# The last layer's first product in Strassen form, with its softplus as one ScalarE function

## The chip, the cores and the metric

The kernel runs on one core of one Trainium2 chip. The metric is the device time of that core in microseconds (us), as the median of several executions. The traces of a profiled execution come from the same core; all times inside a trace count from the first instruction of the span.

## The reference

Three blocks run one after the other. Causal attention (2 batches, 8 heads, 576 positions, head size 64) gives 1152 tokens of 512 numbers. A mixture of eight experts, with weights from an iterated row and column normalisation, follows; each expert is `relu(x @ w1) @ w2` with 1024 hidden columns. The last block is one plain feed-forward layer with 2048 hidden columns and a softplus:

```
def _moe2_ref(x, w_in, w_out):
    h = x @ w_in
    g = np.maximum(h, 0.0) + np.log1p(np.exp(-np.abs(h)))
    return (g @ w_out).astype(np.float32)
```

`x` is 1152 x 512, `w_in` 512 x 2048, `w_out` 2048 x 512. This block and its input are what the change is about.

## The kernel before

**Parts.** Hidden columns are worked in slices of 512, which the code calls layers `x`. The experts are the layers 0 to 15 (`NX` = 16), the last block the layers 16 to 19 (`NH` = 20). A layer has a first product (512 numbers of a token to 512 hidden ones, tile `ph`), an activation (`evict`, to `hh` and `hl`) and a second product (`downs`, tile `py`, accumulated over layers in `acc`).

**Three passes.** Every operand is kept as a high part in the fast matmul type and a low part that holds the rest (`xh`/`xl`, `w1h`/`w1l`, `hh`/`hl`). A product is the sum high x high, high x low, low x high, so each block of a product is three TensorE instructions.

**Experts' first product.** The class `Unit` (L273) works one half `g` of the tokens (576, as two halves of 288 columns) and one half `p` of the hidden columns by Strassen's scheme: seven products `p1` to `p7` of 6 matmuls each (L293), in place of eight. Sums between the products are done by ScalarE copies out of PSUM (L301, `v` and `u`) and VectorE additions (L314, L332, L343). The token columns have seven blocks: `B11`, `B21`, `B22` as they are and `T1` to `T4` as sums; the weights likewise (`sums1`, `sums2` on GpSimd, `split` on ScalarE and VectorE). The experts' eviction is one ScalarE `Relu` (L238) and one VectorE subtraction (L241).

**The last block's first product.** `plain` (L346) makes a hidden block of 128 x 288 by 12 matmuls (L357), four such blocks per `p` and `g`: 48 matmuls where a `Unit` has 42. Its eviction is three ScalarE functions (`Abs`, `Exp`, `Ln`, L253 to L255), two VectorE operations (L259, L260), one on GpSimd (L261), one more on VectorE (L264), then the high part by ScalarE (L267) and the low part by VectorE (L270), put off over the next pieces by `defer` and `flush`.

**Between the two.** The tokens that enter layer 16 are `acc` after layer 15. `turn(g)` (L973) transposes them on TensorE into `px` (L981, L991); ScalarE takes the high part (L983, L992) and VectorE the low part (L985, L994).

**Order.** The work is recorded in the order of strings that `play` reads: `a1` ... `b4` are products of the two units, `p` half a plain block, `d` three matmuls of a second product for one tile of 128 tokens, `=0` to `=2` and `w0` to `w3` start the preparation of the next layer's weights, one step of which follows every piece (`step`). Each engine runs its instructions in that order. Layer `x` plays `A_SEQ` (its own second half of tokens and the second products of tiles 0 to 3), then `B_SEQ` (the next layer's first half, and tiles 4 to 8). From layer 16 on `A_PLAIN` and `B_PLAIN` take their place, and between layers 15 and 16 stands a part of its own, in which `turn(0)` and `turn(1)` are played.

Of the kernel before, what the change touches and what calls it, by code (L numbers as in the profile page):

```python
# [10 lines left out]
F32 = mybir.dt.float32  # L11
# [9 lines left out]
def attention_moe_ffn(ctx, tc, q, k, v, s, w_gate, w1, w2, w_in, w_out, out):  # L21
# [148 lines left out]
    def prep1(x, g):  # L170
# [3 lines left out]
        if g == 0:  # L174
            if x < NX:
                for p in range(2):
                    yield from sums1(x, p)
            for p in range(2):
                yield from split(x, p, 0, [(slice(0, 2), slice(2, 4))])
            if x < NX:  # L180
                for p in range(2):
                    yield from sums2(x, p)
        elif g == 1:
            for p in range(2):
                yield from split(x, p, 1, [(slice(0, 2), slice(1, 3) if x < NX else slice(1, 5, 3))])
                if x >= NX:
                    load(x + 1, 1, p)
        elif x < NX:
# [23 lines left out]
    m3_t = []  # L212
# [20 lines left out]
    def evict(x, k, z, q, cols):  # L233

        hh, hl = hb[0][:, q, cols], hb[1][:, q, cols]
        if x < NX:
# [12 lines left out]
        m3 = m3_t[-1]  # L249
        a1 = m3.tile([P, HB], F32, tag="a1", name="a1")  # L250
        a2 = m3.tile([P, HB], F32, tag="a2", name="a2")
        a3 = m3.tile([P, HB], F32, tag="a3", name="a3")
# [4 lines left out]
        def sums():  # L257

            nc.vector.tensor_scalar(a2, a1, 1.0, -1.0, ALU.add, ALU.add)  # L259
            nc.vector.scalar_tensor_tensor(out=a3, in0=z, scalar=0.0, in1=a3, op0=ALU.max, op1=ALU.add)  # L260
            nc.gpsimd.tensor_tensor(out=a2, in0=a1, in1=a2, op=ALU.subtract)  # L261

        def total_():
            nc.vector.tensor_tensor(out=a3, in0=a3, in1=a2, op=ALU.add)  # L264

        def high():
            nc.scalar.activation(out=hh, in_=a3, func=AF.Copy)  # L267

        def rest_():
            nc.vector.tensor_tensor(out=hl, in0=a3, in1=f(hh), op=ALU.subtract)  # L270

        defer(1, sums)
        defer(3, total_)  # L273
        defer(5, high)
        defer(7, rest_)

# [68 lines left out]

    def plain(x, p, g, i, j):  # L346

        o = ps.tile([P, 512], F32, tag="sc", name="ph", bufs=4)[:, :HB]
        wh, wl = wt[x, 1, p, i]
        ops = []  # L350
        for r in range(2):
            for c in range(2):
                k = slice(c * P, (c + 1) * P)
                h, l = xh[g][:, 2 * r + c, j, :], xl[g][:, 2 * r + c, j, :]
                ops += [(wh[:, r, k], h), (wh[:, r, k], l), (wl[:, r, k], h)]
        for n, (u, v) in enumerate(ops):
            nc.tensor.matmul(o, u, v, start=(n == 0), stop=(n == 11))  # L357
            if n == 5:
                flush()
                yield  # L360
        flush()
        evict(x, 0, o, p + 2 * i, slice(g * S + j * HB, g * S + (j + 1) * HB))
        yield
# [43 lines left out]
    with tc.manual_schedule():  # L407
# [565 lines left out]
        def turn(g):  # L973
# [186 lines left out]
```

## Time and profile before

| what | value |
|---|---|
| median of three runs | 1088.02 us (1087.88 to 1089.03) |
| profiled execution, its own time | 1087.74 us |
| its span, first to last instruction | 1086.0 us |
| TensorE busy | 1071.4 us (99%) |
| VectorE busy | 772.9 us (71%) |
| ScalarE busy | 521.9 us (48%) |
| GpSimd busy | 359.9 us (33%) |
| granted TensorE clock | 0.999 of full speed |

The span is 1.74 us shorter than the profiled execution's time, and that execution lies 0.28 us under the median. Matmuls overlap each other in the trace (one of 288 columns has a duration of 0.30 us, and the next starts 0.13 us after it), so the length of a row of matmuls is read from starts, or from the chain of waits, which merges a row of equal ones to one piece with its length.

### The profile page before, as it was taken

What the parts mean: (1) busy time and instruction counts of PE and PEld (TensorE: products, weight loads), DVE (VectorE), ACT (ScalarE), POOL (GpSimd) and SP (SyncE); (2) the same over time, 40 slices, a digit from 0 to 9 for tenths busy, and PEclk for the clock granted to TensorE, in tenths of its full rate; (3) what the DMA queues carried; (4) which work ended last, traced back from release to release, by engine and by line L of the source; (5) the groups of instructions that cost most, each with busy time, mean ns of one, the idle gap of its engine ahead of it and who ended that gap; (6) DMA issues with size and microseconds to landing.
All of it is one profiled execution on the core that took longest, in us unless ns stands there. A gap on an engine that the chain in (4) does not pass through costs nothing.

```text
span 1086.0 us, 18114 instructions
## 1 busy us (share of the span) xinstructions
PE 1071.4 (99%) x6684; PEld 944.5 (87%) x6684; DVE 772.9 (71%) x1731; ACT 521.9 (48%) x1239; POOL 359.9 (33%) x429
## 2 busy tenths in 40 slices
PE   7999999999999999999999999999999999999998
PEld 4777889889898888988888898888889898989896
DVE  5576556767877878787887888775455568687774
ACT  7998444334443433434343343434333365566661
POOL 8785303053332415134241523423020032323231
PEclk9999999999999999999999999999999999999999
DMA  5221111122232222223222231411112111111002
GB/s 195 85 76 55 40 40 39 40 86 97 92 126 89 85 98 97 94 75 134 83 83 97 98 95 71 136 59 40 39 39 68 50 40 40 39 40 40 1 11 77
DMA packets 30384, 78.43 MB, mean 72 GB/s; under 512 B 5728, under 2 KB 10848, under 8 KB 30296
## 3 DMA queue, kind: packets, MB, share of 16 engines
q1 hardware_dynamic: 27552, 68.69, 18.7%
q0 software_dynamic: 2560, 8.39, 2.0%
q8 instruction: 52, 0.85, 0.3%
q14 instruction: 36, 0.29, 0.1%
q10 hardware_dynamic: 184, 0.20, 0.1%
HBM read 65.99 MB, written 10.75 MB: 71 GB/s over the span
## 4 chain that ended last, share of the span: by engine, by line
PE 93%; DVE 3%; ACT 2%; POOL 1%; issue 1%; DMA 0%; SPq 0%; POOLq 0%; ACTq 0%; DVEq 0%
PE py L382 46%; PE ph L293 32%; PE ph L357 9%; PE sc L598 1%; PE pv L705 1%; PE tr L679 1%; ACT eb L648 1%; POOL eb L661 1%; PE sc L602 0%; PE tr L673 0%; PE pv L715 0%; PE pg L885 0%; ACT pt L693 0%; PE tr L685 0%; PE px L991 0%
## 5 line engine op out<-in xcount | busy, mean ns | idle before, releaser
L382 PE MATMUL py<-w2h,hh 128*128 128x512 f32 x720 | 285.8, 397 | 0.1
L382 PE MATMUL py<-w2h,hl 128*128 128x512 f32 x720 | 284.8, 396 | 1.0 <-DVE hl L241 1.0
L382 PE MATMUL py<-w2l,hh 128*128 128x512 f32 x720 | 284.5, 395 | 0.0
L293 PE MATMUL ph<-xh,w1h 128*128 128x288 f32 x896 | 265.2, 296 | 0.2 <-ACT v L301 0.2
L293 PE MATMUL ph<-xh,w1l 128*128 128x288 f32 x896 | 264.8, 296 | 0.0
L293 PE MATMUL ph<-xl,w1h 128*128 128x288 f32 x896 | 263.4, 294 | 0.0
L293 PEld LDWEIGHTS ph<-xh,w1h 128*128 128x128 f32 x896 | 168.0, 187 | 17.5 <-ACT v L301 0.5
L293 PEld LDWEIGHTS ph<-xl,w1h 128*128 128x128 f32 x896 | 168.3, 188 | 16.5
L293 PEld LDWEIGHTS ph<-xh,w1l 128*128 128x128 f32 x896 | 168.2, 188 | 0.0
L382 PEld LDWEIGHTS py<-w2h,hl 128*128 128x128 f32 x720 | 135.2, 188 | 33.9 <-DVE hl L241 1.6
L238 ACT ACTIVATE hh<-ph 128x288 fp32r<-128x288 f32 x192 | 78.6, 411 | 161.0 <-DVE ph L343 82.2
L204 POOL TENSOR_TENSOR w2l<-raw,w2h 128x512 fp32r<-128x512 f32 x40 | 56.0, 1400 | 290.7 <-ACT w2h L202 290.7
L382 PEld LDWEIGHTS py<-w2h,hh 128*128 128x128 f32 x720 | 135.1, 188 | 12.7 <-DVE acc L400 0.6
L382 PEld LDWEIGHTS py<-w2l,hh 128*128 128x128 f32 x720 | 135.3, 188 | 11.6
L301 ACT ACTIVATE v<-ph 128x288 f32<-128x288 f32 x128 | 50.8, 410 | 172.6 <-PE ph L293 169.7
L400 DVE SCALAR_TENSOR_TENSOR acc<-py,gate,acc 128x512 f32<-128x512 f32 x126 | 94.0, 746 | 53.2 <-PE py L382 53.1
L968 POOL TENSOR_TENSOR cm<-cm,ct 128x512 f32<-128x512 f32 x32 | 45.1, 1408 | 202.5 <-DVE ct L966 202.5
L152 DVE TENSOR_TENSOR w1l<-raw,w1h 128x512 fp32r<-128x512 f32 (+1 forms) x144 | 98.3, 683 | 15.2 <-ACT w1h L149 15.1
L241 DVE SCALAR_TENSOR_TENSOR hl<-ph,hh 128x288 fp32r<-128x288 f32 x192 | 86.7, 454 | 30.7 <-ACT hh L238 29.0
L261 POOL TENSOR_TENSOR a<-a,a 128x288 f32<-128x288 f32 x64 | 51.7, 808 | 125.0 <-DVE a L259 119.8
L149 ACT ACTIVATE w1h<-raw 128x512 fp32r<-128x512 f32 (+1 forms) x144 | 83.0, 576 | 1.6 <-PE ph L293 1.6
L357 PE MATMUL ph<-xh,w1h 128*128 128x288 f32 x256 | 76.0, 297 | 0.0
(191 smaller groups left out, 1692.1 us busy)
## 6 DMA issues: line engine op xcount, KB each, us to landing
raw<-in_w SPq DMA_DIRECT2D x64, 512.0 KB
f<-in_w_in SPq DMA_DIRECT2D x16, 512.0 KB
f<-in_w_out SPq DMA_DIRECT2D x16, 512.0 KB
wd<-cm POOLq DMA_DIRECT2D x32, 256.0 KB, 3.1
raw<-wd SPq DMA_DIRECT2D x16, 512.0 KB
out<-acc SPq DMA_DIRECT2D x9, 256.0 KB
vv<-in_v SPq DMA_DIRECT2D x8, 256.0 KB
qk<-in_k SPq DMA_DIRECT2D x7, 288.0 KB
```

Of the source, the lines that this page charges most:

```text
L149: nc.scalar.activation(out=hi[:, o], in_=t[:, src], func=AF.Copy)
L152: nc.vector.tensor_tensor(out=lo[:, o], in0=t[:, src], in1=f(hi[:, o]), op=ALU.subtract)
L204: (nc.gpsimd if i else nc.vector).tensor_tensor(out=lo, in0=t[:, r], in1=f(hi), op=ALU.subtract)
L238: nc.scalar.activation(out=hh, in_=z, func=AF.Relu)
L241: nc.vector.scalar_tensor_tensor(out=hl, in0=z, scalar=0.0, in1=f(hh), op0=ALU.max, op1=ALU.subtract)
L261: nc.gpsimd.tensor_tensor(out=a2, in0=a1, in1=a2, op=ALU.subtract)
L293: nc.tensor.matmul(o, u, v, start=(start and c == 0 and n == 0), stop=(c == 1 and n == 2), skip_group_check=True)
L301: nc.scalar.activation(out=t, in_=self.a, func=AF.Copy)
L357: nc.tensor.matmul(o, u, v, start=(n == 0), stop=(n == 11))
L382: nc.tensor.matmul(py[t], u, v, start=(k == 0 and n == 0), stop=(k == NF - 1 and n == 2))
L400: nc.vector.scalar_tensor_tensor(out=a, in0=py, scalar=gate_t[0][:, t, e:e + 1], in1=a, op0=ALU.mult, op1=ALU.add)
L968: nc.gpsimd.tensor_tensor(out=m, in0=m, in1=f(t), op=ALU.add)
```

## The change

The four layers of the last block use `Unit` as the experts do, and `plain` with its two sequences is gone. `evict` for these layers is a `Softplus` of ScalarE in place (in PSUM, or in the tile `t`), a ScalarE `Copy` to `hh` and a VectorE subtraction to `hl`. A table set with softplus is loaded once, ahead of layer 14. `turn` builds seven blocks per half `g` and is cut in two: its first part (`t`) transposes into a tile `xq` and makes `B11` and `B21`, its second (`u`) the sums `T1` to `T4` and `B22`. The sequence `TURN` plays these among layer 15's second products and layer 16's first ones, and `A_TURN` follows it. The preparation of the weights treats all layers alike.

```diff
@@ prep1 @@
-            if x < NX:
-                for p in range(2):
-                    yield from sums1(x, p)
+            for p in range(2):
+                yield from sums1(x, p)
...
@@ evict @@
         hh, hl = hb[0][:, q, cols], hb[1][:, q, cols]
-        if x < NX:
-            def high():
+
+        def high():
+            if x < NX:
                 nc.scalar.activation(out=hh, in_=z, func=AF.Relu)
-
-            def rest_():
+            else:
+                nc.scalar.activation(out=z, in_=z, func=AF.Softplus)
+                nc.scalar.activation(out=hh, in_=z, func=AF.Copy)
+
+        def rest_():
+            if x < NX:
                 nc.vector.scalar_tensor_tensor(out=hl, in0=z, scalar=0.0, in1=f(hh), op0=ALU.max, op1=ALU.subtract)
-
-            if k < 0:
-                high()
             else:
-                defer(k, high)
-            defer(k + 1, rest_)
-            return
...
-        nc.scalar.activation(out=a1, in_=z, func=AF.Abs)
-        nc.scalar.activation(out=a1, in_=a1, func=AF.Exp, scale=-1.0)
-        nc.scalar.activation(out=a3, in_=a1, func=AF.Ln, bias=1.0)
...
+                nc.vector.tensor_tensor(out=hl, in0=z, in1=f(hh), op=ALU.subtract)
+
+        if k < 0:
+            high()
+        else:
+            defer(k, high)
+        defer(k + 1, rest_)
...
@@ turn @@
+        def rows(g, cs, tiles, o):
+
+            n = len(tiles) * P
+            px = ps.tile([P, len(cs), n], F32, tag="tr", name="px", bufs=2)
+            for i, c in enumerate(cs):
+                for j, t in enumerate(tiles):
+                    nc.tensor.transpose(px[:, i, j * P:(j + 1) * P], acc[0][:, t, c * P:(c + 1) * P], ident)
+            nc.scalar.activation(out=xq_t[g][:, cs[0]:cs[-1] + 1, o:o + n], in_=px, func=AF.Copy)
...
+        def both_parts(g, blk, src):
+            h, l = xh[g][:, blk], xl[g][:, blk]
+            for c in range(2):
+                nc.scalar.activation(out=h[:, c, :] if isinstance(blk, int) else h[:, :, c, :], in_=src(c), func=AF.Copy)
+            yield
+            for c in range(2):
+                o = (l[:, c, :], h[:, c, :]) if isinstance(blk, int) else (l[:, :, c, :], h[:, :, c, :])
+                nc.vector.tensor_tensor(out=o[0], in0=src(c), in1=f(o[1]), op=ALU.subtract)
+            yield
+
+        def turn(g, first):
+
+            if first:
+                xq_t[g] = tq_[0].tile([P, KD, S], F32, tag="xq", name="xq", bufs=1)
+            xq = xq_t[g]
+            if first:
+                if g:
+                    rows4(g)
+                    yield
+                for cs in ((0, 1), (2, 3)) if g else ((0,), (1,), (2,), (3,)):
+                    rows(g, cs, (NB + 1, NB + 2) if g else range(NB), REM if g else 0)
+                    yield
+                yield from both_parts(g, B11, lambda c: xq[:, c, :HB])
+                yield from both_parts(g, B21, lambda c: xq[:, c + 2, :HB])
+                return
+            if g:
+                for cs in ((0, 1), (2, 3)):
+                    rows(g, cs, (NB + 3, NB + 4), REM + 2 * P)
+                    yield
+            else:
+                rows4(g)
                 yield
+            xt = [tq_[0].tile([P, 4, HB], F32, tag=f"xt{c}", name="xt", bufs=1) for c in range(2)]
+
+            def sum_(c, n):
+                x1, x2 = xq[:, c, :], xq[:, c + 2, :]
+                o, a, b = [(0, x1[:, HB:], x1[:, :HB]), (1, x2[:, HB:], xt[c][:, 0, :]), (3, x2[:, :HB], xt[c][:, 1, :]),
+                           (2, x2[:, HB:], x1[:, HB:])][n]
+                (nc.gpsimd if n == 3 else nc.vector).tensor_tensor(out=xt[c][:, o, :], in0=a, in1=b, op=ALU.subtract)
+
+            for c in range(2):
+                for n in (3, 0, 1, 2):
+                    sum_(c, n)
+            yield
+            yield from both_parts(g, slice(T2, T3 + 1), lambda c: xt[c][:, 1:3, :])
+            yield from both_parts(g, B22, lambda c: xq[:, c + 2, HB:])
+            for z in (T1, T4):
+                yield from both_parts(g, slice(z, z + 1), lambda c: xt[c][:, z - T1:z - T1 + 1, :])
...
@@ play @@
+                if z[0] in "tu":
+                    side.append(turn(int(z[1]), z[0] == "t"))
+                    continue
...
-        A_PLAIN = "p p p p d d p d p d p d p d =0 p d p d p d p d p d p d p d p =1 d d d"
+        A_TURN = "a1 b1 a2 b2 =0 d d d d a6 d b6 d a7 d b7 =1 d a5 d b5 d a3 d b3 d a4 d b4 d d d"
+        TURN = ("t0 d d d d u0 d d d d d a1 d b1 d a2 d =2 b2 t1 d a6 d b6 d a7 d b7 d a5 d b5 d d u1 w0 a3 w2 b3 w1 a4 w3 b4")
...
-                m3_t.append(ctx.enter_context(tc.tile_pool(name="m3", bufs=6, reuse_waits="tile")))
-            play(A_SEQ if x < NX else A_PLAIN, products(x, 1), downs(x, A_GROUPS))
+                nc.scalar.preload_act_table_set("softplus")
+            play(A_SEQ if x != NX else A_TURN, products(x, 1), downs(x, A_GROUPS))
...
+            if x + 1 == NX:
+                tq = ctx.enter_context(tc.tile_pool(name="tq", bufs=1, reuse_waits="tile"))
+                tq_.append(tq)
+                play(TURN, products(NX, 0), d)
+            elif x + 1 < NH:
                 play(B_SEQ, products(x + 1, 0), d)
...
```

Three places show how instructions move. On TensorE, where the tokens' transposes begin, before:

```order
L382 MATMUL py<-w2h_9185,hh 128x512
L382 MATMUL py<-w2l_9186,hh 128x512
L382 MATMUL py<-w2h_9185,hl 128x512
L981 MATMUL px<-ident,acc 128x64 x4
L382 MATMUL py<-w2h_9203,hh 128x512
L382 MATMUL py<-w2l_9204,hh 128x512
L382 MATMUL py<-w2h_9203,hl 128x512
L991 MATMUL px<-ident,acc 128x128 x4
```

The same place on TensorE in the changed kernel, just after layer 15's tiles 0 to 3 are complete (L337 is the old L382, L936 the old L991):

```order
L337 MATMUL py<-w2h_9242,hl 128x512
L337 MATMUL py<-w2h_9183,hh 128x512
L337 MATMUL py<-w2l_9184,hh 128x512
L337 MATMUL py<-w2h_9183,hl 128x512
L936 MATMUL px<-ident,acc 128x128 x4
L337 MATMUL py<-w2h_9201,hh 128x512
```

Before, the first transposes are of the shared tile 4 and stand after its second product; now they are of tiles 0 to 3 and stand one `d` into tile 4, whose own transposes come four `d` and more later.

On ScalarE, evictions of the last block before (L253 to L255 softplus, L267 the high part):

```order
L253 ACTIVATE a_10207<-ph 128x288
L254 ACTIVATE a_10207<-a_10207 128x288
L255 ACTIVATE a_10209<-a_10207 128x288
L267 ACTIVATE hh<-a_10175 128x288
L253 ACTIVATE a_10239<-ph 128x288
```

On ScalarE in the changed kernel, from the first blocks of half 0 on (L937 and L946 take transposes to `xq`, L951 a block's high part, L275 the copies `v`, L236 and L237 softplus and high part):

```order
L937 ACTIVATE xq<-px 128x512 x4
L951 ACTIVATE xh_74<-xq 128x288 x4
L946 ACTIVATE xq<-px 128x4x64
L275 ACTIVATE v<-ph 128x288
L951 ACTIVATE xh_74<-xt 128x2x288 x2
L275 ACTIVATE v<-ph 128x288
L951 ACTIVATE xh_74<-xq 128x288 x2
L236 ACTIVATE ph<-ph 128x288
L237 ACTIVATE hh<-ph 128x288
L951 ACTIVATE xh_74<-xt 128x288 x2
```

Four functions per evicted block have become two, and the blocks' high parts stand in the same queue as the first evictions of layer 16.

On VectorE, from the first low part of the tokens on, before:

```order
L985 TENSOR_TENSOR xl_76<-px,xh_74 128x4x64
L994 TENSOR_TENSOR xl_76<-px,xh_74 128x512 x2
L400 SCALAR_TENSOR_TENSOR acc<-py,gate,acc 128x512
L994 TENSOR_TENSOR xl_76<-px,xh_74 128x512 x2
L400 SCALAR_TENSOR_TENSOR acc<-py,gate,acc 128x512
L204 TENSOR_TENSOR w2l_9547<-raw_9230,w2h_9546 128x512
```

The same in the changed kernel (L986 are the sums to `xt`, L955 the low parts, L355 the old L400, L288 the sum in `p2`, L243 the eviction's low part):

```order
L955 TENSOR_TENSOR xl_76<-xq,xh_74 128x288 x2
L355 SCALAR_TENSOR_TENSOR acc<-py,gate,acc 128x512
L955 TENSOR_TENSOR xl_76<-xq,xh_74 128x288 x2
L986 TENSOR_TENSOR xt<-xq 128x288
L986 TENSOR_TENSOR xt<-xq,xt 128x288 x2
L986 TENSOR_TENSOR xt<-xq 128x288
L986 TENSOR_TENSOR xt<-xq,xt 128x288 x2
L955 TENSOR_TENSOR xl_76<-xt,xh_74 128x2x288 x2
L288 TENSOR_TENSOR ph<-ph,v 128x288
L955 TENSOR_TENSOR xl_76<-xq,xh_74 128x288 x2
L355 SCALAR_TENSOR_TENSOR acc<-py,gate,acc 128x512
L243 TENSOR_TENSOR hl<-ph,hh 128x288
```

The sums and the two-block low parts now stand ahead of the addition of `p2` and of the eviction that frees its bank.

## Rows read from the trace of the kernel before

**Rows 1.** The page: busy time, share of the span, instructions.

```profile
PE 1071.4 (99%) x6684; PEld 944.5 (87%) x6684; DVE 772.9 (71%) x1731; ACT 521.9 (48%) x1239; POOL 359.9 (33%) x429
```

**Rows 2.** The page: chain that ended last, shares by line.

```profile
PE py L382 46%; PE ph L293 32%; PE ph L357 9%; PE sc L598 1%; PE pv L705 1%; PE tr L679 1%; ACT eb L648 1%; POOL eb L661 1%; PE sc L602 0%; PE tr L673 0%; PE pv L715 0%; PE pg L885 0%; ACT pt L693 0%; PE tr L685 0%; PE px L991 0%
```

**Rows 3.** Waits of PE and PEld, 820 to 1086 us: total, times, longest.

```profile
PE px L981 <- DVE acc L400: 0.2, 1, 0.2
...
PEld py L382 <- DVE acc L400: 0.6, 1, 0.6
PEld px L981 <- DVE acc L400: 0.6, 1, 0.6
```

**Rows 4.** Waits of PE, 120 to 820 us.

```profile
PE py L382 <- DVE hl L241: 1.0, 1, 1.0
```

**Rows 5.** Chain of waits: start, length; the five products between two expert layers.

```profile
599.60 3.99 PE ph L293 x30
...
837.00 3.99 PE ph L293 x30
```

**Rows 6.** The same, where two layers of the last block meet, and the end.

```profile
941.12 4.76 PE ph L357 x36
...
1042.40 4.76 PE ph L357 x36
...
1065.83 16.11 PE py L382 x69
```

**Rows 7.** Chain of waits, 858 to 872 us, where `turn(0)` is played.

```profile
858.74 4.21 PE py L382 x18
...
862.98 0.76 DVE acc L400
...
863.79 0.46 PE px L981 x4
...
865.14 0.44 PE px L991 x4
...
871.11 0.76 DVE acc L400
...
871.92 0.95 PE py L382 x3
```

**Rows 8.** Instructions that touch tile `ph`: duration ns min/median/max, first and last start.

```profile
L238 ACT ACTIVATE hh<-ph x192: 389/411/415, 111.2 to 859.3; 128x288 fp32r<-128x288 f32 x192
L241 DVE SCALAR_TENSOR_TENSOR hl<-ph,hh x192: 443/454/460, 111.6 to 859.7; 128x288 fp32r<-128x288 f32 x192
```

**Rows 9.** Groups by line and shape, 941.12 to 1042.40 us: busy, mean ns.

```profile
L267 ACT ACTIVATE hh<-a 128x288 fp32r<-128x288 f32 x33 | 14.4, 436 | 18.7 <-DVE a L264 18.7
L255 ACT ACTIVATE a<-a 128x288 f32<-128x288 f32 x32 | 14.3, 445 | 1.0
```

**Rows 10.** VectorE's line L270, whose two inputs lie in SBUF: duration min/median/max.

```profile
L270 DVE TENSOR_TENSOR hl<-a,hh x64: 444/725/1016, 882.2 to 1071.4; 128x288 fp32r<-128x288 f32 x64
```

**Rows 11.** Timeline of VectorE, 893 to 895 us: start, duration.

```profile
893.14 0.45 DVE L264 TENSOR_TENSOR a<-a,a 128x288 f32<-128x288 f32 x1
...
894.09 1.01 DVE L270 TENSOR_TENSOR hl<-a,hh 128x288 fp32r<-128x288 f32 x1
```

**Rows 12.** Timeline of GpSimd, the same stretch.

```profile
893.98 0.81 POOL L261 TENSOR_TENSOR a<-a,a 128x288 f32<-128x288 f32 x1 [1.29 <-DVE a L259]
```

**Rows 13.** Timeline of ScalarE, 0 to 4 us.

```profile
2.46 1.28 ACT L479 ACT_TABLE_LOAD   x1 [2.46 <-issue]
```

**Rows 14.** Timeline of VectorE, 858 to 861 us: end of layer 15's first product.

```profile
858.78 0.47 DVE L343 TENSOR_TENSOR ph<-ph,u 128x288 f32<-128x288 f32 x1
859.73 0.46 DVE L241 SCALAR_TENSOR_TENSOR hl<-ph,hh 128x288 fp32r<-128x288 f32 x1 [0.48 <-ACT hh L238]
860.18 0.75 DVE L400 SCALAR_TENSOR_TENSOR acc<-py,gate,acc 128x512 f32<-128x512 f32 x1
```

**Rows 15.** Windows of an expert layer and of the last block: PE, PEld, DVE, ACT, POOL.

```profile
786.00:829.00 43.00, 43.00 (x253) 38.67 (x252) 21.64 (x42) 15.64 (x36) 8.42 (x10) 1.00 0.14 50
...
958.00:1001.00 43.00, 43.00 (x256) 38.77 (x255) 31.12 (x62) 23.65 (x57) 13.11 (x15) 1.00 0.15 50
```

More of the change, by code (lines that the diff above doesn't have):

```diff
@@ L174, in prep1 @@
         if g == 0:
-            if x < NX:
-                for p in range(2):
-                    yield from sums1(x, p)
+            for p in range(2):
+                yield from sums1(x, p)
             for p in range(2):
                 yield from split(x, p, 0, [(slice(0, 2), slice(2, 4))])
-            if x < NX:
-                for p in range(2):
-                    yield from sums2(x, p)
+            for p in range(2):
+                yield from sums2(x, p)
         elif g == 1:
             for p in range(2):
[L185 to L188, printed above, removed]
+                yield from split(x, p, 1, [(slice(0, 2), slice(1, 3))])
+        else:
             for p in range(2):
@@ L211, in attention_moe_ffn @@
     m_t = []
-    m3_t = []
     hb = []
@@ L344, in p4 @@
             evict(self.x, 0, self.c, self.p + 2, self.h0)
[L346 to L363, printed above, removed]
     def downs(x, groups):
@@ L984, in turn @@
             yield
[L985 removed]
+            for c in range(2):
+                o = (l[:, c, :], h[:, c, :]) if isinstance(blk, int) else (l[:, :, c, :], h[:, :, c, :])
+                nc.vector.tensor_tensor(out=o[0], in0=src(c), in1=f(o[1]), op=ALU.subtract)
             yield
[L987 to L995 removed]
+        def turn(g, first):
[16 more added lines that the diff above has]
+                    yield
+            else:
+                rows4(g)
+                yield
+            xt = [tq_[0].tile([P, 4, HB], F32, tag=f"xt{c}", name="xt", bufs=1) for c in range(2)]
[12 more added lines that the diff above has]
+                yield from both_parts(g, slice(z, z + 1), lambda c: xt[c][:, z - T1:z - T1 + 1, :])
@@ L999, in attention_moe_ffn @@
         back = []
+        side = []
         tick = [0, 0, 0, 0]
@@ L1015, in step @@
                 next(conv, None)
-            while back and next(back[0], 1):
-                back.pop(0)
+            for todo in (back, side):
+                while todo and next(todo[0], 1):
+                    todo.pop(0)
         def rest():
-            for z in back:
-                for _ in z:
-                    pass
-            back.clear()
+            for todo in (back, side):
+                for z in todo:
+                    for _ in z:
+                        pass
+                todo.clear()
         ORDER = "a1 b1 a2 b2 a6 b6 a7 b7 a5 b5 a3 b3 a4 b4"
         def products(x, g):
-            if x < NX:
-                u = dict(a=Unit(x, 0, g), b=Unit(x, 1, g))
-                return {z: getattr(u[z[0]], "p" + z[1]) for z in ORDER.split()}
-            def sums():
-                for i in range(2):
-                    for j in range(2):
-                        for p in range(2):
-                            yield from plain(x, p, g, i, j)
-            z = sums()
-            return {"p": lambda: next(z)}
+            u = dict(a=Unit(x, 0, g), b=Unit(x, 1, g))
+            return {z: getattr(u[z[0]], "p" + z[1]) for z in ORDER.split()}
         def play(seq, todo, d=None):
```

57 lines of the change are left out of this document (5 added, 52 removed).

## The prediction, made before the changed kernel ran

> **What bounds the kernel now.** I read the page's busy shares first: TensorE is busy 99% of the span, no other engine above 71% [rows 1]. The chain that ended last then says whether this is work or overlap: the second products (L382) hold 46% of it, the experts' first product (L293) 32%, the last block's first product (L357) 9%, and no line of another engine more than 1% [rows 2]. TensorE's own waits come third, since a full engine can still stand still at one place. From 120 to 820 us, nearly all of the expert layers, it waited 1.0 us once [rows 4]; from 820 us to the end its queue for weights shows two waits of 0.6 us and its matmuls one of 0.2, all for VectorE's update of `acc`, around the transposes [rows 3]. So from 120 us on the time is TensorE's count of instructions times their pitch. A matmul removed there is worth its pitch, and other work matters only where it makes TensorE wait.
>
> **The gain: 24 matmuls in each of four layers.** A plain half layer has 48 matmuls per `p`, a `Unit` 42, so a layer has 4 x 6 = 24 fewer, four layers 96. I price them in two ways. By the pitch: 36 matmuls of the last block follow each other in 4.76 us, 0.132 each [rows 6], so 96 make 12.7 us. By whole layers, which holds everything that differs between the forms: the piece where two expert layers meet starts at 599.60 and again, five layers on, at 837.00 [rows 5], 47.48 us per layer; the piece where two layers of the last block meet starts at 941.12 and, two layers on, at 1042.40 [rows 6], 50.64 us. The difference, 3.16 us, times four is 12.64 us. I take 12.64. Second products, transposes (40 of them in `turn` before and after) and the last 69 matmuls [rows 6] are the same in both kernels, and so is what follows the last matmul.
>
> **Evictions in the four layers.** Before, a block had four ScalarE functions of about 0.44 us [rows 9], four VectorE operations and one on GpSimd. Now a `Unit` half layer has, as with the experts, four evictions and three copies, and an eviction is two ScalarE functions. No row shows Softplus, nor a ScalarE write into PSUM. Bounds from near rows: `Relu` out of PSUM 0.41, `Ln` 0.445 [rows 8, 9], and as the far end `Abs`, `Exp`, `Ln` together, 1.3 us. I take 0.45, as all ScalarE functions of this size shown lie within 0.04 of each other. The Trainium skill (ScalarE: Activation LUTs, section "Step-by-step: what each stage is for") says that ScalarE takes the same time per element whatever the function; rows 8 and 9 agree for four of them, none shows Softplus.
>
> An expert layer keeps ScalarE busy 15.64 of 43 us [rows 15]. Sixteen extra functions of 0.45 per layer add 7.2, so ScalarE stays near half full. What counts is the longer chain at the end of a layer's first product. In layer 15 the last matmul of `b4` ends about 858.74 [rows 7]; VectorE adds at 858.78, then `Relu`, and the low part is done at 859.73 + 0.46 = 860.19 [rows 14]. One more function makes it 860.65. Its first reader is the fourth `d` of tile 4, two `d` of tile 3 and three of tile 4 after `b4`: 858.74 + 5 x 0.70 = 862.24, with 0.70 for three matmuls (16.11 us for 69, [rows 6]). So 1.5 us of cover is left of 2.0, and I price it at nothing. Without that cover it would be one stall per layer of the length by which the chain is late.
>
> **The table load.** One more load of a ScalarE table, ahead of layer 14; a load took 1.28 us at the start [rows 13]. Behind it ScalarE has the last `Relu` of the layer before and the copies `v`, which `a6` needs: three products of 0.79 and two `d` later, 3.8 us. Price nothing; on the path it would be at most 1.28.
>
> **The turn, where the cost is.** Before, `turn(0)` cost TensorE two stops: its matmul queue was at work until about 863.48 and the first transpose came at 863.79; the last weight before 871.92 had gone out by 871.61 [rows 7]. That is 0.3 us each, 0.6 in all, and both places go: the first transposes now wait only for tile 3, whose update ends at 860.93 [rows 14], while one `d` from 859.98 runs to 860.68; and the paired group of tiles 7 and 8 that waited for a bank of `py` is two single groups. What comes late next is the handing on of blocks. I lay them out from `t0` at 859.98:
>
> - Four `d` with four sets of transposes (0.44 each, [rows 7]), five more `d` and the small set: `a1` starts about 868.5. `B11` and `B21` are two ScalarE functions and two VectorE ones each; they queue from 865.2 on and are done about 867.3. No wait.
> - The sums start with the copy of the small set, 868.8: six on VectorE, two on GpSimd, then low parts of two blocks at once. `a6` reads them four products and three to four `d` after 868.5, at about 874.4. At 0.45 a VectorE operation (starts 0.37 apart) they are done at 872.6.
> - But all six read two SBUF tiles while GpSimd reads SBUF too. L270, of the same kind, has a minimum of 444 and a median of 725 ns [rows 10], and one beside a GpSimd operation of 0.81 [rows 12] took 1.01 where its neighbour took 0.45 [rows 11]: 0.56 more per meeting, 1.1 us for two, up to 1.6 if the two engines take strict turns. Then the low parts are done at 873.7 to 874.2, just ahead of `a6`, and the additions and evictions of `a2` and `b2` queue behind them; these free the two PSUM banks that the next two sets of transposes take. By this reckoning TensorE stops three times, 0.4 to 0.5 each.
>
> The Trainium skill (SBUF — State Buffer, section "Who interferes with whom") says that a VectorE instruction with two SBUF inputs and a GpSimd instruction that reads SBUF exclude each other. By it each meeting would cost VectorE up to the whole 0.81, 3.2 us for the turn's four GpSimd sums; by rows 11 it is 0.56, 2.2 us. I go by the rows; the rule speaks for the high end of the stalls.
>
> As a check, VectorE's whole work in `TURN`, counted from the order: 38 operations of 288 columns (0.45), two of 576 (at most 0.9), some eight of 512 (0.75) and two small ones: 25.6 us, with the meetings up to 27.8. TensorE has 20 `d`, 14 products and ten sets of transposes, 14.0 + 11.1 + 4.4 = 29.5 us. VectorE is nearly full, in part waiting for ScalarE in order, so some stops are likelier than none. Bounds for them: nothing, and 4 us, if each of the ten pairs of low parts in the two halves made TensorE stop for 0.4. I take 1.4, the three stops of the layout. Half 1 has more cover: its `B11` stands ready long before `a1`, and four `d` in a row stand before `a6`.
>
> **Sum.** Against the profiled execution: 1087.74 - 12.64 - 0.6 + 1.4 = 1075.9. The median is 0.28 above that execution, so 1076.2 is the forecast.
>
> **Rivals.**
>
> 1. *VectorE becomes the bound in the turn.* For it: 27.8 of 29.5 us, and rows 10 with over half of such operations stretched. Against it: the work is spread, and the late blocks (`T1`, `T4`, `B22`) have five products of cover. If the stops reach 4 to 7 us in the two halves, the time is 1088.02 - 12.64 - 0.6 + 4 to 7 = 1079 to 1082.
> 2. *The longer eviction chain shows at every seam.* For it: 0.45 of 2.0 us of cover goes, and ScalarE has weight splits in the same queue. Against it: experts' layers ran with no wait [rows 4]. If each of seven seams lost 0.5 to 1 us: 3.5 to 7 us more, 1079.7 to 1083.
> 3. *Softplus is slow and ScalarE becomes the bound; slower than before.* An expert layer has 47.48 us; ScalarE needs about 15.64 x 47.48/43 = 17.3 of it, and 7.2 for the second functions. What is left, 23 us over 16 evictions, is 1.4 us each: from 1.9 us per function on, a layer is ScalarE's. To eat 12.64 us over four layers takes 3.2 us more per layer, so about 2.1 us per function; at 2.5 us the time is 1076.2 + 64 x 0.6 = 1115. Against it: every function shown takes 0.41 to 0.445, and the order has one table load, not one per function.
> 4. *The change doesn't do what it says*: the products are 42, but the copies and sums between them stop TensorE, so that a layer stays near 50.6 us. Against it stands the expert layers' 47.48 us in the same code. It would end near 1088.
>
> **How the numbers follow.** What this kernel's measurement can tell from no change is about 0.2%, 2.2 us. The forecast gets 0.80, with a range of its own from 1074.7 (no stop at all: 1088.02 - 12.64 - 0.6) to 1078.8 (stops of 4 us). Rival 1 gets 0.10, rival 2 0.05, rival 3 0.03, rival 4 0.01; 0.01 is left for a gain beyond the count. The range 1074.5 to 1079.0 leaves out most of rivals 1 to 4. All but rivals 3 and 4 are faster by over 0.2%: faster 0.96, within 0.2% 0.01, slower 0.03.
>
> **What would show it.** The seams of layers 16 to 19 should be 47.5 us apart; Softplus about 0.45 us; TensorE's waits should stand only between 860 and 890 us, below 3 us in all, on VectorE (banks, low parts) or ScalarE (`xq` copies) before `px`; GpSimd's sums there should go with VectorE sums stretched to about 1 us. The forecast is wrong if seams of the last layers lie over 48 us apart, or if the waits in the turn exceed 4 us.

## The result, and the profile after

The changed kernel took 1078.16 us, the median of 4 runs (1078.05 to 1079.39), against 1087.95 (1087.88 to 1089.03, 4 runs) for the kernel before: ratio 0.991, 95% interval 0.9893 to 0.9927. It is 9.8 us faster, where 11.8 were forecast. The profiled execution took 1078.05 us with a span of 1076.3 and a granted clock of 1.0; the sum had said 1075.9, so 2.15 us are missing. Executions of one kernel, of before too, lie in two groups some 1.1 us apart, and in the profiled ones the difference arises ahead of layer 15's seam (836.8 to 838.1 us), so small effects are read below from a stretch behind it.

The page's busy times, answering to [rows 1], and the chain by line, answering to [rows 2]:

```profile
PE 1059.6 (98%) x6588; PEld 931.5 (87%) x6588; DVE 727.7 (68%) x1629; ACT 504.5 (47%) x1200; POOL 336.4 (31%) x401
...
PE py L337 45%; PE ph L267 39%; PE sc L553 2%; PE pv L660 1%; PE tr L634 1%; DVE xt L986 1%; DVE xl L955 1%; PE sc L557 1%; POOL eb L616 1%; PE tr L628 1%; PE pv L670 0%; PE pg L840 0%; PE tr L640 0%; ACT eb L603 0%; PE px L936 0%
```

TensorE has 96 matmuls fewer, as counted, and is still what the chain consists of. New in the chain are VectorE's `xt` (L986, the sums `T1` to `T4`) and `xl` (L955, the low parts of the tokens): both belong to `turn`.

The chain of waits of the changed kernel at the seams of layers 15, 17, 18 and 19 and at the end (start, length), answering to [rows 5] and [rows 6]:

```profile
836.91 3.99 PE ph L267 x30
...
940.13 3.99 PE ph L267 x30
987.61 3.99 PE ph L267 x30
1035.09 3.99 PE ph L267 x30
...
1056.83 15.41 PE py L337 x66
```

From layer 17 on the seams are 47.48 us apart, where 50.64 stood in [rows 6]. Up to layer 15's seam nothing moved (836.91, before 837.00). The 66 second products at the end have the pitch they had (15.41 us for 66; 16.11 for 69 in [rows 6]). So what is missing was lost between 836.91 and 940.13, in the turn. TensorE's waits there, in its weights' queue (820 to 1077 us; total, times, longest), answering to [rows 3]:

```profile
PEld py L337 <- DVE acc L349: 1.5, 1, 1.5
PEld py L337 <- DVE hl L243: 0.9, 1, 0.9
PEld px L936 <- DVE hl L243: 0.5, 1, 0.5
PEld px L944 <- DVE hl L243: 0.5, 1, 0.5
PEld py L337 <- DVE w2l L200: 0.4, 1, 0.4
PEld px L944 <- issue: 0.4, 1, 0.4
PEld px L936 <- ACT xq L946: 0.3, 1, 0.3
PEld px L936 <- DVE acc L355: 0.2, 1, 0.2
```

The timeline of the weights' queue gives their places (start, duration, in brackets the idle time before and what ended it):

```profile
876.27 0.32 PEld L944 LDWEIGHTS px<-ident,acc 64*128 64x128 f32 x4 [0.51 <-DVE hl L243]
...
878.00 0.42 PEld L936 LDWEIGHTS px<-ident,acc 128*128 128x128 f32 x4 [0.52 <-DVE hl L243]
...
879.26 0.42 PEld L936 LDWEIGHTS px<-ident,acc 128*128 128x128 f32 x4 [0.35 <-ACT xq L946]
...
896.37 0.19 PEld L337 LDWEIGHTS py<-w2h,hl 128*128 128x128 f32 x1 [0.91 <-DVE hl L243]
...
898.67 0.19 PEld L337 LDWEIGHTS py<-w2l,hh 128*128 128x128 f32 x1 [0.41 <-DVE w2l L200]
...
905.93 0.19 PEld L337 LDWEIGHTS py<-w2h,hh 128*128 128x128 f32 x1 [1.49 <-DVE acc L349]
```

Two clusters: three stops at 876 to 879, where half 1's first transposes wait for what half 0's blocks hold up (half 0's stops from here on), which the forecast had; and three at 896 to 906, half 1's, which it had not. They are 1.38 and 2.81 us, 4.19 in all. Two smaller ones, 0.36 us at 868 and 0.20 at 887, make up the rest of the list. The worst, 1.49 us, waits for a copy out of `py` (L349) that stands in VectorE's queue behind half 1's low parts. VectorE there:

```profile
890.81 0.97 DVE L986 TENSOR_TENSOR xt<-xq 128x288 f32<-128x288 f32 x1
891.88 2.35 DVE L986 TENSOR_TENSOR xt<-xq,xt 128x288 f32<-128x288 f32 x2
894.15 0.45 DVE L986 TENSOR_TENSOR xt<-xq 128x288 f32<-128x288 f32 x1
894.64 0.95 DVE L986 TENSOR_TENSOR xt<-xq,xt 128x288 f32<-128x288 f32 x2
...
898.90 1.93 DVE L955 TENSOR_TENSOR xl<-xq,xh 128x288 fp32r<-128x288 f32 x2
900.75 0.45 DVE L288 TENSOR_TENSOR ph<-ph,v 128x288 f32<-128x288 f32 x1
901.12 0.44 DVE L243 TENSOR_TENSOR hl<-ph,hh 128x288 fp32r<-128x288 f32 x1
901.48 1.36 DVE L955 TENSOR_TENSOR xl<-xt,xh 128x288 fp32r<-128x288 f32 x2
...
903.13 1.54 DVE L955 TENSOR_TENSOR xl<-xt,xh 128x288 fp32r<-128x288 f32 x2
904.60 0.68 DVE L152 TENSOR_TENSOR w1l<-raw,w1h 128x512 fp32r<-128x512 f32 x1
905.20 0.68 DVE L349 COPY acc<-py 128x512 f32<-128x512 f32 x1
```

And GpSimd in the same stretch:

```profile
890.66 1.79 POOL L986 TENSOR_TENSOR xt<-xq 128x288 f32<-128x288 f32 x2 [19.58 <-DVE hl L243]
892.41 1.51 POOL L200 TENSOR_TENSOR w2l<-raw,w2h 128x512 fp32r<-128x512 f32 x1
899.22 1.30 POOL L200 TENSOR_TENSOR w2l<-raw,w2h 128x512 fp32r<-128x512 f32 x1 [5.30 <-ACT w2h L198]
900.47 0.96 POOL L158 TENSOR_TENSOR raw<-raw 128x256 f32<-128x256 f32 x1
...
903.52 0.84 POOL L160 TENSOR_TENSOR raw<-raw 128x256 f32<-128x256 f32 x1
```

Each slow VectorE row lies beside a GpSimd row; the two at 894.15 and 894.64, with no GpSimd beside them, take 0.45 and 0.95 for two. With 0.45 for one, 0.95 for a pair of sums and 0.82 for a pair of low parts undisturbed, VectorE lost 0.52 + 1.40 + 1.11 + 0.54 + 0.72 = 4.3 us here. Only operations whose inputs both lie in SBUF are slow here: the two at 900.75 and 901.12 have one input in PSUM (`ph`), lie beside GpSimd too, and take 0.45 and 0.44. That the meetings are what makes TensorE stop is a reading so far; the experiments test it.

### The profile page after: what moved, and what is told of

It is laid out like the page before. It is cut to its first block, busy times and chain, and to the rows that moved or that the text cites. A ratio compares the mean times of both kernels' runs of the same rounds, so it can differ in the third digit from the quotient of the medians.

```text
span 1076.3 us, 17617 instructions
## 1 busy us (share of the span) xinstructions
PE 1059.6 (98%) x6588; PEld 931.5 (87%) x6588; DVE 727.7 (68%) x1629; ACT 504.5 (47%) x1200; POOL 336.4 (31%) x401
## 4 chain that ended last, share of the span: by engine, by line
PE 92%; DVE 4%; ACT 2%; issue 1%; POOL 1%; DMA 0%; POOLq 0%; ACTq 0%; DVEq 0%
PE py L337 45%; PE ph L267 39%; PE sc L553 2%; PE pv L660 1%; PE tr L634 1%; DVE xt L986 1%; DVE xl L955 1%; PE sc L557 1%; POOL eb L616 1%; PE tr L628 1%; PE pv L670 0%; PE pg L840 0%; PE tr L640 0%; ACT eb L603 0%; PE px L936 0%
## 5 line engine op out<-in xcount | busy, mean ns | idle before, releaser
L267 PE MATMUL ph<-xh,w1h 128*128 128x288 f32 x1120 | 331.6, 296 | 0.3 <-ACT v L275 0.3
L267 PE MATMUL ph<-xh,w1l 128*128 128x288 f32 x1120 | 331.0, 295 | 0.0
L267 PE MATMUL ph<-xl,w1h 128*128 128x288 f32 x1120 | 329.2, 294 | 0.0
L337 PE MATMUL py<-w2h,hh 128*128 128x512 f32 x720 | 285.9, 397 | 1.3 <-DVE acc L349 1.3
L337 PE MATMUL py<-w2h,hl 128*128 128x512 f32 x720 | 284.8, 396 | 1.4 <-DVE hl L241 1.0
L337 PE MATMUL py<-w2l,hh 128*128 128x512 f32 x720 | 284.6, 395 | 0.1
L267 PEld LDWEIGHTS ph<-xh,w1h 128*128 128x128 f32 x1120 | 209.9, 187 | 21.7 <-ACT v L275 0.5
L267 PEld LDWEIGHTS ph<-xl,w1h 128*128 128x128 f32 x1120 | 210.3, 188 | 20.6
L267 PEld LDWEIGHTS ph<-xh,w1l 128*128 128x128 f32 x1120 | 210.3, 188 | 0.0
L337 PEld LDWEIGHTS py<-w2h,hl 128*128 128x128 f32 x720 | 135.3, 188 | 34.9 <-DVE hl L241 1.6
L275 ACT ACTIVATE v<-ph 128x288 f32<-128x288 f32 x160 | 63.5, 409 | 212.8 <-PE ph L267 209.8
L337 PEld LDWEIGHTS py<-w2h,hh 128*128 128x128 f32 x720 | 135.2, 188 | 13.5 <-DVE acc L349 1.5
L337 PEld LDWEIGHTS py<-w2l,hh 128*128 128x128 f32 x720 | 135.3, 188 | 12.1 <-DVE w2l L200 0.4
L355 DVE SCALAR_TENSOR_TENSOR acc<-py,gate,acc 128x512 f32<-128x512 f32 x126 | 94.0, 746 | 56.9 <-PE py L337 56.7
L149 ACT ACTIVATE w1h<-raw 128x512 fp32r<-128x512 f32 (+1 forms) x160 | 91.3, 571 | 0.0
L306 DVE TENSOR_TENSOR t<-ph,v 128x288 f32<-128x288 f32 x80 | 36.3, 454 | 72.9 <-ACT v L275 72.3
L198 ACT ACTIVATE w2h<-raw 128x512 fp32r<-128x512 f32 x80 | 50.6, 632 | 13.6 <-PE py L337 12.8
```

Source lines behind the costliest of these rows:

```text
L149: nc.scalar.activation(out=hi[:, o], in_=t[:, src], func=AF.Copy)
L198: nc.scalar.activation(out=hi, in_=t[:, r], func=AF.Copy)
L267: nc.tensor.matmul(o, u, v, start=(start and c == 0 and n == 0), stop=(c == 1 and n == 2), skip_group_check=True)
L275: nc.scalar.activation(out=t, in_=self.a, func=AF.Copy)
L306: defer(0, lambda: nc.vector.tensor_tensor(out=t, in0=self.c, in1=u4, op=ALU.add))
L337: nc.tensor.matmul(py[t], u, v, start=(k == 0 and n == 0), stop=(k == NF - 1 and n == 2))
```

## The experiments

Two theories of why half 1 stops. **A**: meetings with GpSimd (the turn's sums, low parts of layer 16's second weights `w2l`, sums of layer 17's first weights) make VectorE late. **B**: VectorE's queue stands in order behind ScalarE's longer chain of evictions, whatever GpSimd does. Small effects are read from the stretch from layer 15's seam to layer 17's seam: 103.22 us in the changed kernel (940.13 - 836.91). It is one profiled execution for each kernel; how far to trust it shows in the two layers behind it, which are 47.48 us each in the changed kernel and in every experiment on it but the one with matmuls given back. "Less" is against 103.22.

**GpSimd's two sums per half moved to VectorE.**

```diff
-                (nc.gpsimd if n == 3 else nc.vector).tensor_tensor(out=xt[c][:, o, :], ...)
+                nc.vector.tensor_tensor(out=xt[c][:, o, :], ...)
```

> The changed kernel with the turn's four GpSimd sums on VectorE instead. Theory A (VectorE's queue is late in the turn, and its meetings with GpSimd stretch it): in the changed kernel the six VectorE sums of half 0 take 3.7 us and of half 1 4.7 us; eight sums at 0.37 take 3.0. VectorE is earlier by 0.7 and 1.7 us, TensorE's stops fall by 1 to 2 us, the time to 1076.2 to 1077.2. Theory B (the longer eviction chain, two ScalarE functions one after the other, makes the stops): the chain is untouched and VectorE has four operations more; 1078.0 to 1078.6.

Measured: 1078.45 us, ratio 0.9909 (0.9892 to 0.9925), stretch 102.81: 0.41 less than the changed kernel. The time lies in B's range, and the gain is under the 1 to 2 us of A. GpSimd's timeline shows why:

```profile
891.03 1.29 POOL L200 TENSOR_TENSOR w2l<-raw,w2h 128x512 fp32r<-128x512 f32 x1 [39.67 <-ACT w2h L198]
898.98 1.29 POOL L200 TENSOR_TENSOR w2l<-raw,w2h 128x512 fp32r<-128x512 f32 x1 [6.66 <-ACT w2h L198]
```

The first low part moved up to 891.03, into the place of the sums, and met VectorE's block sums instead, the first pair of which takes 1.92 us where 0.83 is the undisturbed value:

```profile
890.71 1.92 DVE L986 TENSOR_TENSOR xt<-xq 128x288 f32<-128x288 f32 x2
```

A meeting was traded, not removed, and VectorE has two sums more per half.

**Layer 16's first partial sum copied by ScalarE.**

```diff
-            nc.vector.tensor_copy(a, py)
+            nc.scalar.activation(out=a, in_=py, func=AF.Copy)
```

> The changed kernel with layer 16's nine copies of py to acc on ScalarE instead of VectorE. The longest stop of TensorE, 1.4 us at 905.9 us, ends with such a copy. Theory A: the copy was late only because it stands in VectorE's queue behind the low parts of half 1; on ScalarE the bank comes free 1.5 us or more earlier, the stop goes, 1076.6 to 1077.2. Rival: TensorE would next wait for what stands before the copy in the same queue (weights' or tokens' low parts); the stop turns into another, 1077.6 to 1078.3.

Measured: 1077.48 us, ratio 0.9898 (0.9883 to 0.9912), stretch 101.73: 1.49 less. The median lies between A's range and the rival's; the waits decide: the line on `acc` L349 is gone from the weights' queue, and the other seven are those of the changed kernel.

The stop of 1.49 us was worth its whole length, and it was VectorE's lateness and not the data: `py` was ready, since ScalarE could copy it in time.

**`t1` three products later in `TURN`.**

```diff
-  ... =2 b2 t1 d a6 d b6 d a7 d b7 d a5 ...
+  ... =2 b2 d a6 d b6 d a7 d t1 b7 d a5 ...
```

> The changed kernel with half 1's first part of the turn started four pieces later (after a7 instead of after b2), so that its transposes take PSUM banks that the evictions of a2 and b2 have freed long before. Theory A: the three stops in half 0 (0.5, 0.5, 0.35 us) go, half 1's stay as they are: 1076.7 to 1077.3. Rival C: half 1's blocks come later by as much and its stops grow; 1077.8 to 1078.8.

Measured: 1077.5 us, ratio 0.9899 (0.9885 to 0.9914), stretch 102.55: 0.67 less. All three stops of half 0 are gone (0.16 us remains, on a weight's low part); half 1's stay: 1.0, 0.4 and 1.5 us. So half 1's stops don't come from half 0's, and of the 1.38 us that the queue shows for half 0, 0.67 was time lost.

**The three together.** No new edit.

> The three edits together. Theory A: nearly all stops (3.7 us by the trace) go: 1074.6 to 1075.6. If only VectorE's total load mattered, the gains of the three would overlap and it ends at 1076 to 1077. Theory B: 1077 or more.

Measured: 1076.73 us, ratio 0.989 (0.9875 to 0.9905), stretch 101.38: 1.84 less, not the sum of the three (2.57), and not A's forecast: the median is in the range for gains that overlap. What is left in half 1: 0.9 for `hl`, 0.5 for `acc`, whose copy now comes late from ScalarE, and 0.4 for `w2l`.

**One Relu in place of Softplus and Copy** (the softplus is left out, so only the time counts).

```diff
-                nc.scalar.activation(out=z, in_=z, func=AF.Softplus)
-                nc.scalar.activation(out=hh, in_=z, func=AF.Copy)
+                nc.scalar.activation(out=hh, in_=z, func=AF.Relu)
```

> The changed kernel with the last block's Softplus and Copy replaced by one Relu out of the bank (the softplus is left out of the computation). Theory A: an eviction chain shorter by 0.43 us frees banks and low parts a little earlier; of 3.7 us of stops at most 1 goes: 1077.1 to 1078.1. Theory B (the longer chain makes the stops): 1074.8 to 1076.0. Seams of layers 17 to 19 stay 47.48 us apart under both.

Measured: 1078.18 us, ratio 0.9903 (0.9888 to 0.9918), stretch 102.44: 0.78 less. The `hl` stop falls from 0.9 to 0.3 us and two of half 0's shrink (to 0.25 and 0.18), but the one on `acc` (L348 here) stays, at 1.7 us. The longer eviction chain has a share, and it is the smaller one.

**The matmuls given back**: in layers 17 to 19 each `p7` is done twice, 72 matmuls more.

```diff
-            self.product(self.c, S3, T3, True)
+            for _ in range(2 if self.x > NX else 1):
+                self.product(self.c, S3, T3, True)
```

> The changed kernel with the product p7 done twice in layers 17 to 19 (the second time from zero again): 12 half layers x 6 = 72 matmuls more, nothing else. If a matmul in these layers is worth its pitch of 0.132 us: + 9.5 us, 1087.6, seams 3.17 us further apart. If they had hidden waits that a longer product could fill: less, 1082 to 1086.

Measured: 1088.06 us, ratio 0.9996 (0.9987 to 1.0006); the profiled execution took 1087.50, 9.45 more than that of the changed kernel. Its chain at the seams of layers 17 and 19:

```profile
941.62 3.99 PE ph L267 x30
...
1042.94 3.99 PE ph L267 x30
```

Two layers apart, 50.66 us per layer, 3.18 more for 24 matmuls, 0.132 each: the gain is the count of matmuls.

**The new eviction alone**, in the kernel before: Softplus in place, Copy, one subtraction, no Strassen form.

```diff
-        nc.scalar.activation(out=a1, in_=z, func=AF.Abs)
...
+            nc.scalar.activation(out=z, in_=z, func=AF.Softplus)
+            nc.scalar.activation(out=hh, in_=z, func=AF.Copy)
...
+            nc.vector.tensor_tensor(out=hl, in0=z, in1=f(hh), op=ALU.subtract)
```

> The kernel before with one part of the change alone: plain products of 48 matmuls, but the eviction by Softplus in place, Copy and one subtraction. My theory (TensorE's count sets the time, evictions are covered): 1087.6 to 1088.2, no change. Rival (the four-function eviction with its GpSimd step cost time): 1085 to 1087.

Measured: 1088.69 us against 1088.67 for the kernel before beside it, ratio 1.0 (0.999 to 1.001). Fewer operations on three engines that were already hidden buy nothing.

**Layer 17's weights started later in `A_TURN`.**

```diff
-        A_TURN = "a1 b1 a2 b2 =0 d d d d a6 d b6 ..."
+        A_TURN = "a1 b1 a2 b2 d d d d a6 =0 d b6 ..."
```

> The changed kernel with one edit in the sequence A_TURN: layer 17's weight sums on GpSimd (=0) start after a6 instead of after b2, five pieces later. In the changed kernel VectorE's low parts of T1 and T4 in half 1 stand beside these GpSimd sums and take 1.36 and 1.54 us for a pair that takes 0.82 alone, and layer 16's copy of py stands behind them. If GpSimd's meetings make VectorE late: 1.2 us less on VectorE, the 1.4 us stop at that copy shrinks to 0.2 to 0.4, the stretch from layer 15's seam to layer 17's goes from 103.22 to 102.0 to 102.3. If VectorE's order alone makes it late: no change, 103.2.

Measured: 1078.19 us, ratio 0.9906 (0.989 to 0.9923), stretch 102.62: 0.60 less. It didn't separate the theories: GpSimd's sums of weights still began at 900.8 us, since their place in the program moved but nothing they wait for did. The gain has another cause: the copy L349 now stands ahead of the weights' low part, and its stop is 0.9 us in place of 1.5.

**All four edits** (the three together, and the weights later).

> The kernel with all three earlier edits (stretch 101.38) and the weights' sums later as well. The 0.5 us wait for ScalarE's copy of py should go, since the evictions ahead of it on ScalarE wait for VectorE; the waits for the low part of a4's eviction (0.9 in the weights' queue) and for GpSimd-stretched w2l (0.4) stay: stretch 101.0 to 101.3, time 0.2 to 0.4 us under e4's. If nothing is left to gain there: 101.4.

Measured: 1076.23 us (1075.73 to 1076.88), ratio 0.9888 (0.9873 to 0.9903), stretch 100.88: 2.34 less than the changed kernel. This is the fastest version that computes the whole, ahead of both kernels. Two of half 1's stops are left, 0.9 for `hl` and 0.4 for `w2l`.

**GpSimd quiet.**

```diff
-        (nc.gpsimd if i else nc.vector).tensor_tensor(out=lo, in0=t[:, r], in1=f(hi), op=ALU.subtract)
+        if i and x == NX:
+            nc.scalar.activation(out=lo, in_=t[:, r], func=AF.Copy)
...
+                if n == 3:
+                    nc.scalar.activation(out=xt[c][:, o, :], in_=a, func=AF.Copy)
...
+        if x == NX + 1:        # sums1; sums2 of layer 17 do nothing
+            nc.scalar.activation(out=t[:, 0], in_=t[:, 4], func=AF.Copy)
```

> The changed kernel with GpSimd's work around the second half of layer 16 taken off GpSimd: the turn's sums that GpSimd made are ScalarE copies of one of their terms, the low parts of layer 16's second weights are ScalarE copies of the high parts, and layer 17's first weights' sums are left out but for one ScalarE copy. So parts of the computation are left out or changed, and only its time is to be read. Theory A, meetings with GpSimd make VectorE late in half 1: VectorE's block sums and low parts there (0.97 to 0.94 us of GpSimd-stretched pairs at 1.9 to 2.35 us, 1.36 to 1.93 us for pairs of low parts) run at 0.4 us apiece, VectorE is some 3 us earlier when it comes to the copy of layer 16's first partial sum, that stop of 1.5 us and the 0.9 and 0.4 us before it go, and the stretch from layer 15's seam to layer 17's seam falls from 103.2 us to 101.0 to 101.6 us. Theory B, VectorE is late because its queue stands in order behind ScalarE's chain from the last block's evictions, whatever GpSimd does: the stops stay and the stretch is 102.7 us or more. Half 0's three stops stay by both, for VectorE's sums there meet one GpSimd pair alone, or shrink by one at most.

Measured: 1075.2 us, ratio 0.9882 (0.9865 to 0.9898), stretch 936.85 - 837.00 = 99.85: 3.37 less than the changed kernel. All that its weights' queue still waits for:

```profile
PEld px L956 <- DVE xl L967: 0.4, 1, 0.4
PEld px L956 <- issue: 0.4, 1, 0.4
PEld px L948 <- DVE acc L367: 0.2, 1, 0.2
```

VectorE, the rows that answer to those of the changed kernel (L1001 is the sums, L967 the low parts, L361 the copy):

```profile
890.10 0.45 DVE L1001 TENSOR_TENSOR xt<-xq 128x288 f32<-128x288 f32 x1
890.65 0.95 DVE L1001 TENSOR_TENSOR xt<-xq,xt 128x288 f32<-128x288 f32 x2
...
896.27 0.82 DVE L967 TENSOR_TENSOR xl<-xq,xh 128x288 fp32r<-128x288 f32 x2
...
901.31 0.69 DVE L152 TENSOR_TENSOR w1l<-raw,w1h 128x512 fp32r<-128x512 f32 x1 [0.63 <-ACT w1h L149]
901.92 0.68 DVE L361 COPY acc<-py 128x512 f32<-128x512 f32 x1
```

VectorE has the same operations to do as in the changed kernel, ScalarE has more (63.0 us busy against 57.7, 837 to 942 us), and yet half 1's three stops are gone; the 0.2 us at 887 is in the changed kernel too. That is A, and more of it than A expected. The copy comes at 901.92 in place of 905.20. Half 0 was expected to keep its stops; two of three went there too and the third shrank to 0.37. VectorE needs 4.43 us from its first sum to the low part of `B22` there (869.05 to 873.48), 5.41 in the changed kernel (868.97 to 874.38): 0.98 us for one pair of GpSimd sums.

**Only layer 17's weight sums left out** (the `sums1` and `sums2` part of the edit above alone).

> The changed kernel with only layer 17's first weights' sums on GpSimd left out (one ScalarE copy stands for them), so part of the computation is left out and only its time is to be read. In the changed kernel four of them run from 900.5 to 904.4 us beside VectorE's pairs of low parts that take 1.36 and 1.54 us there for 0.82 undisturbed. If meetings are what costs, these two pairs fall to 0.82 each, VectorE comes to the copy of layer 16's first partial sum 1.2 us earlier and that stop of 1.5 us falls to 0.3 us or less; the stops for the low part (0.9) and the second weights (0.4) before it stay, for their meetings are with the turn's sums and the second weights' low parts: stretch 102.0 to 102.3 us. If the order of VectorE's queue behind ScalarE is what costs: 103 us, nothing changed.

Measured: 1078.92 us, ratio 0.9916 (0.99 to 0.9933), stretch 102.85: 0.37 less, where A said 0.9 to 1.2. VectorE's rows:

```profile
903.87 0.83 DVE L964 TENSOR_TENSOR xl<-xt,xh 128x288 fp32r<-128x288 f32 x2
905.33 0.69 DVE L152 TENSOR_TENSOR w1l<-raw,w1h 128x512 fp32r<-128x512 f32 x1 [0.63 <-ACT w1h L149]
905.94 0.68 DVE L358 COPY acc<-py 128x512 f32<-128x512 f32 x1
```

The pairs fell to 0.83 (the one shown) and 0.81 as A said, but then VectorE stood 0.63 us waiting for ScalarE's `w1h`, with the copy queued behind: the stop went from 1.5 to 1.0 us only. This wait is no proof of B, for the edit makes it: ScalarE's copies that stand for the sums come ahead of `w1h` in its queue,

```profile
903.09 0.41 ACT L159 ACTIVATE raw<-raw 128x256 f32<-128x256 f32 x1
...
904.07 0.41 ACT L159 ACTIVATE raw<-raw 128x256 f32<-128x256 f32 x1
```

and put back what follows by 0.31 us each: `w1h` begins 66.65 us after layer 15's seam (904.67), 66.02 in the changed kernel (902.93). Without these 0.62 us the gain would be about 1.0, as A said; this is an estimate and was not run.

**Only layer 16's second weights' low parts by ScalarE** (the `lo` part of the edit alone).

> The changed kernel with only layer 16's second weights' low parts that GpSimd made replaced by ScalarE copies, so part of the computation is changed and only its time is to be read. By the meetings it gains little: GpSimd no longer waits 5.3 us for ScalarE between two of them, so layer 17's weights' sums, which nothing else holds, run some 8 us earlier, from about 892.5 us, beside VectorE's block sums, and trade one set of meetings for another: stops stay 1.5 us or more in half 1, stretch 102.3 to 103.3 us. If it were the low parts' own meetings alone that made VectorE late (about 1.1 us at 898.9 and 0.5 us at 892.4), the stretch would be 101.6 us or less.

Measured: 1077.76 us, ratio 0.9907 (0.9892 to 0.9922), stretch 102.78: 0.44 less, in the range that trading gives. Layer 17's sums moved up and took the free place beside VectorE's block sums, the stop on `hl` grew from 0.9 to 1.8 us, and the one on `acc` shrank to 0.2:

```profile
892.39 0.96 POOL L158 TENSOR_TENSOR raw<-raw 128x256 f32<-128x256 f32 x1
893.43 0.83 POOL L160 TENSOR_TENSOR raw<-raw 128x256 f32<-128x256 f32 x1
```

So taking away one of GpSimd's jobs gains 0.4 us each time (0.41, 0.37, 0.44; sum 1.2), and all three 3.4 us. In two of the three single edits the trace shows the next job moving up into the gap; in the third the edit's own copies on ScalarE eat part of the gain. The three edits aren't quite the parts of the whole one, which has the sums on ScalarE and not on VectorE.

## Why the prediction was right or wrong

- **The gain, 12.64 us: right.** The layer period went from 50.64 to 47.48 us exactly as read from the experts' layers, and giving 72 of the 96 matmuls back gave 9.45 us back, 0.131 each.
- **Softplus 0.45 us, evictions and the table load at nothing: right.** Softplus took 395 ns in place in PSUM (48 of them) and 445 in the tile `t` (16); the load took 1.28 us at 790.12. From 906 us on TensorE waits for nothing, and from 120 to 820 us for one 1.0 us as in [rows 4]. The eviction alone, in the kernel before, changed nothing. In the turn, though, the second function is not free: one Relu in place of the two takes 0.78 us off the stretch. (Rows 8 and 9 show three functions and not four; in the same stretch the trace of before has `Abs` at 0.404 and `Exp` at 0.445 us, so the reading stands.)
- **The two old stops, 0.6 us: right.** TensorE's queue has no wait before 868 us in the turn.
- **Half 0's stops: right in place, number and size in the queue, too dear in time.** Three before `px`, 0.51, 0.52 and 0.35 us (forecast three of 0.4 to 0.5, sum 1.4). With `t1` later the three are gone and 0.67 us is gained, so 1.4 was about twice what they cost. The reason given holds for the first two, which wait for evictions of half 0; the third waits for ScalarE's copy of the transposes before it. A meeting costs VectorE 0.49 us there, from the 0.98 for two, where [rows 11] and [rows 12] had given 0.56. The Trainium skill (SBUF — State Buffer, section "Who interferes with whom") has VectorE contend with GpSimd where VectorE's instruction has two SBUF inputs and GpSimd's reads SBUF, which the runs bear out; a full block for the other's whole 0.81 us they don't show.
- **"Half 1 has more cover": this step failed.** Its blocks do stand ready earlier, but the sum counted as meetings only the turn's four GpSimd sums (2.2 us over both halves). In half 1 GpSimd also makes `w2l` and layer 17's weight sums; it is busy 11.47 us from 890 to 910 us, and VectorE lost 4.3 us there alone. The two lines of the first fence below are the windows 860 to 890 and 890 to 910 us of the changed kernel (PE, PEld, DVE, ACT, POOL), the line in the second fence is the second window with GpSimd quiet:

```profile
860.00:890.00 30.00, 29.63 (x180) 25.24 (x179) 21.09 (x43) 19.67 (x49) 2.07 (x2) 1.00 0.10 36
890.00:910.00 20.00, 18.20 (x108) 15.84 (x107) 18.73 (x32) 13.36 (x34) 11.47 (x12) 1.00 0.15 54
```

```profile
890.00:910.00 20.00, 20.00 (x123) 18.23 (x123) 16.04 (x36) 16.92 (x43) 0.00 (x0) 1.00 0.16 54
```

  VectorE is busy 18.73 of 20 us in half 1, and TensorE 18.20; with GpSimd quiet VectorE does more instructions in 16.04 and TensorE is full. So rival 1 (VectorE becomes the bound in the turn) was the right mechanism for half 1, at less than its price. The term "new stops 1.4" measured 1.4 + 2.15 = 3.55 us: about 0.7 for half 0 and 2.9 for half 1, which had been put at nothing. "Below 3 us, between 860 and 890" was wrong on both counts, and the six stops' 4.19 us in the weights' queue pass the 4 us that the prediction named as a sign of being wrong.
- **That the time fell into the range is in part luck.** Its upper end, 4 us of stops, came from ten pairs of low parts that each stop TensorE for 0.4. Nothing like that happened; a bound made for another reason covered half 1. (Its lower end, 1088.02 - 12.64 - 0.6, is 1074.8 and not 1074.7.)
- **What stood behind the waiting instruction was not named.** The largest stop was for the copy L349, whose data was ready; it is a layer's first partial sum, queued behind half 1's low parts and a weight's low part.
- **Rivals 2, 3 and 4**: no seam stops, Softplus is as short as the other functions, and the layers are 47.48 us apart. None came.

Open: how GpSimd's share divides among its three kinds of work, since they trade places when one is taken away, and what the longer eviction chain costs apart from the meetings. A kernel that computes the whole with GpSimd quiet in the turn, its work made to wait for later data, wasn't tried; the stretch of 99.85 us, with work left out, lies 1.0 us under that of the fastest version (100.88).

## What to carry to other kernels

Before giving an engine new work at one place, list all that every engine sharing a resource with it does in that stretch, the run-ahead work of the next stage included, and not only what the change brings. A job with nothing to wait for moves up into a gap, so taking away one job can trade one meeting for another, as it did here twice: test by taking all away at once, and look at what the stand-ins of a test put into other queues. Look for short operations with ready data (here a copy that frees a PSUM bank) queued behind long ones on the late engine, and give them to another engine.

## What the runs showed of the hardware that was not expected

- GpSimd is stretched by the meetings too, but not always: its 64 sums of 128x288 in the kernel before took 0.80 to 0.82 us, the one of [rows 12] beside a stretched VectorE operation too; the four in the turn took 0.81 to 1.08 (median 1.02). Its two `w2l` in half 1 took 1.51 and 1.30, where the median of all 40 is 1.30.
- A VectorE operation of 288 columns was stretched up to 1.56 us (a low part, L955), more than the 1.02 of [rows 10], where it met one GpSimd operation after another. Operations with one input in PSUM kept their 0.44 to 0.47 us beside GpSimd.
- The same ScalarE function on 288 columns takes 395 ns in place in PSUM and 445 ns in place in SBUF; `Relu` from PSUM to SBUF lies between, 411 [rows 8], nearer to the first, so where it reads counts for more than where it writes.
